# A second-largest expert of 320 rows, and weight remainders split between VectorE and GpSimd

## The chip, the cores and the metric

The kernel runs on one core of one Trainium2 chip. The metric is device time in microseconds of one execution; the times shown are the median of three runs, with their lowest and highest. Traces come from one execution under the hardware profiler.

## The reference

Three layers follow each other, all in float32. Pooled attention turns q, k, v (2 batches, 8 heads, 1152 places, 64 dimensions) into 1152 tokens of 512 numbers. A mixture of experts sends each token to one of 8 experts. A last feed-forward layer has 2048 hidden units.

```python
e_idx = np.argmax(x @ w_gate, axis=1)
gate_w = probs[np.arange(N), e_idx]          # softmax of the logits
eom = 1.0 / (1.0 + np.exp(-(x @ w_output_gate)))
for e in range(E):
    mask = e_idx == e
    h = np.maximum(x[mask] @ w1[e], 0.0)     # 512 -> 1024
    ye = h @ w2[e]                           # 1024 -> 512
    out[mask] = gate_w[mask, None] * eom[mask, e, None] * ye
# last layer, on all tokens
h = x @ w_in                                 # 512 -> 2048
sp = np.where(h > 20.0, h, np.log1p(np.exp(np.minimum(h, 20.0))))
return (h * np.tanh(sp)) @ w_out             # 2048 -> 512
```

With the reference's inputs the eight experts get 374, 267, 240, 69, 63, 61, 51 and 27 tokens, sorted by count.

## The kernel before

The program has four parts in order of time: attention (to about 295 us), the routing (to about 316 us), the experts (to about 467 us) and the last feed-forward layer (to the end). The order of all instructions is the order in which the Python code emits them; each engine works off its own list, and semaphores join the lists.

**Precision.** Most matrix products are made of three matmuls in a fast one-pass format (`float32r`): an operand a is split into a rounded part (hi, by ScalarE) and a remainder (lo, by VectorE or GpSimd: `tt(eng, lo, w, hi, subtract)`), and hi x hi, lo x hi and hi x lo are added up (`mm3`, lines 825 to 827). Where few rows are at stake, plain float32 matmuls are used without a split; the trace records each of them as two.

**Experts.** The experts are ranked by count on the chip, and the program has one slot for each rank. `CAP` gives each rank's room in units of 64 rows: (6, 6, 4, 2, 1, 1, 1, 1). Tokens beyond a slot's room go to up to 9 overflow slots, which run only if needed (none ran in the profiled execution). The slots are visited in the order of ranks 0, 3, 4, 1, 5, 2, 6, 7. Ranks 0, 1, 2 are wide slots (`wide_slot`), the others narrow ones (`narrow_slot`), those of 64 rows with plain float32 matmuls whose two halves of 64 output rows each fill one half of the array (`mm2_half`, line 846).

A wide slot is a pipeline of ten steps. Step i < 8 makes hidden units 128 i to 128 i + 127 for all the slot's rows (12 matmuls, as many columns as the slot has rows, into the tile `hps`, of which there are two), then ScalarE takes the ReLU (`hh`) and VectorE its remainder (`hl`). Step i >= 2 also multiplies hidden tile i - 2 by the second layer, for each column tile of 128 rows three matmuls of 512 columns into its tile `yp`. In each step the weights of a later step are split: `w1h` and `w2h` by ScalarE, `w2l` by VectorE, `w1l` by VectorE for the first three and by GpSimd after that. Besides, in rank 1's slot two parts of the decoding of the last layer's weights (`dm`, `ds`, `wd`) run per step on ScalarE and VectorE, from raw data (`wraw`) that ScalarE's queue fetches. At the end ScalarE evicts `yp` and GpSimd scatters the rows.

The slots' weights come as four loads of 1 MB each (`wt`, line 788) on SP's queue, in order, into five buffers; a load waits for the last reader of the buffer that it takes.

**Last layer.** 48 steps: three blocks b of 384 tokens, 16 tiles f of hidden units. In step i of the loop TensorE makes z of tile i (12 matmuls of 384 columns, `zps`) and the output product of tile i - 4 (9 matmuls of 512 columns, `ops`, line 1265); between them lies the activation, in this order on the engines (offset from i):

```python
order_ = [(-4, z_lo), (-1, z_exp), (-3, z_gate), (-2, z_inv), (-2, z_newton),
          (-1, z_num), (2, split_lo), (-3, z_hi), (3, split_hi)]
```

VectorE's list of a step is thus: gl (`z_lo`), the gate (n from n and `zps` in PSUM), l, l, n (`z_newton`), n from u (`z_num`), and in the first block the remainder of a weight tile (`split_lo`, named wd in the trace since it goes into a buffer of the decoded weights). GpSimd clamps u (`ts(G, u, ...)` in `z_num`); ScalarE does exp, ln, exp, gh and the rounded weight (`split_hi`). The first four weight tiles (`NPRE`) are split during the experts; tiles 4 to 15 in the first block. In steps 8, 10, 12 of a block VectorE also scales a tile of the next block's tokens (yt), and in 9, 11, 13 TensorE transposes it and VectorE takes its remainder (yl, from PSUM).

Before the first step the experts' last results stand in three PSUM banks (`yb`); ScalarE and VectorE split them into yh and yl (`ysplit`). The pools of the last layer's PSUM tiles (`ops`, `zps`, `tps`) are opened after the experts' pools are closed, and take over their banks. A tile pool that is opened with `reuse_waits="tile"` makes a new tile wait for the readers and writers of just the old tile whose place it takes; without it, as these three are here, it waits for more of the closed pool.

Of the kernel before, what the change touches and what calls it, by code (L numbers as in the profile page):

```python
# [20 lines left out]
P = 128  # L21
# [11 lines left out]
CAPW = 3  # L33
CAP = (6, 6, 4, 2, 1, 1, 1, 1)
# [50 lines left out]
def kernel(ctx, tc, cst, qt, kt, v, wgo, w1, w2, wio, out):  # L85
# [824 lines left out]
    def wide_slot(s, cks):  # L910
        n = len(cks) * P

        def xprep(j):
            if j == 0:
                xh[s] = mp_.tile([P, 4, n], F32R, name="xh")
                xl[s] = mp_.tile([P, 4, n], F32R, name="xl")
            ps = xpose(cks[j], *(((yps, "yp") if s == slots[0][0] else (fp[0], f"yb{j - 1}")) if j else ()))
            js = slice(j * P, (j + 1) * P)
            act(xh[s][:, :, js], ps)
            tt(V, xl[s][:, :, js], ps, xh[s][:, :, js].bitcast(F32), ALU.subtract)  # L920
# [13 lines left out]
        def main(i):  # L934
            if i < 8:
                ps = hps.tile([P, 4, P], F32, name="hps").rearrange("p a b -> p (a b)")
                a, b_ = w1s[s, i]
                apart = s == slots[0][0] and i == 0 and n > 256
                if apart:

                    for cs_ in (slice(0, 256), slice(256, n)):
                        for u, x_ in ((a, xh), (b_, xh), (a, xl)):
                            for k in range(4):
                                mm(ps[:, cs_], lhsT=u[:, k], rhs=x_[s][:, k, cs_], start=u is a and x_ is xh and k == 0, stop=x_ is xl and k == 3)
                for k in range(4) if not apart else ():
# [12 lines left out]
    def narrow_slot(s, c, m=P):  # L958
# [32 lines left out]
        def main(i):  # L991
# [75 lines left out]
    allc = [(c, min(P, 64 * CAP[p_])) for p_, cks in slots for c in cks]  # L1067
# [288 lines left out]
```

## Time and profile before

| | us |
|---|---|
| three timed runs: median (lowest to highest) | 695.81 (694.01 to 698.62) |
| the profiled execution: time | 697.16 |
| the profiled execution: span of the trace | 695.4 |
| TensorE matmuls busy | 649.5 (93%) |
| VectorE busy | 523.1 (75%) |
| ScalarE busy | 370.8 (53%) |
| GpSimd busy | 140.1 (20%) |
| mean granted clock of TensorE | 0.981 |

Busy shares are means over stages with different limits; a stage is read from its own stretch of the trace. A row of a timeline gives start, duration, engine, line, operation, output and inputs, shape, count of merged instructions, and in brackets the idle time before it with the engine that ended it. Matmuls overlap, so the distance of two starts is what counts, not the duration.

### The profile page before, as it was taken

The page shows a single profiled execution, that of the slowest core. Times are in us where ns is not written, and L with a number is a line of the kernel's source. Part 1 is how long each engine was busy: PE and PEld are TensorE (multiplying, and loading weights), DVE is VectorE, ACT ScalarE, POOL GpSimd, SP SyncE. Part 2 cuts the span into 40 slices and gives each one's busy share as a digit, 9 for nine tenths or more (in the row PEclk, how much of TensorE's full clock was granted, in tenths as well). Part 3 has the DMA queues.
Part 4 walks back from the last instruction along what each step waited for, and adds up shares of the span by engine and source line. Part 5 has one row for each costly group of instructions (what it writes and reads, how often), then busy time and mean ns, then how long its engine had stood idle before and what let it go on. Part 6 is the DMA issues. An engine that isn't in the chain of part 4 may idle for free. (4 is left out here: it accounts for less than half of the span.)

```text
span 695.4 us, 11495 instructions
## 1 busy us (share of the span) xinstructions
PE 649.5 (93%) x4335; PEld 503.6 (72%) x4335; DVE 523.1 (75%) x1035; ACT 370.8 (53%) x753; POOL 140.1 (20%) x139
## 2 busy tenths in 40 slices
PE   5899999999999999858989999988899999999997
PEld 3666666666767666527876977758688899999995
DVE  6897979797979796965743976613999977897775
ACT  6656474747474737514344546523666554555543
POOL 5310000000000000023222424301222332233322
PEclk9999999999999999969999999998999999999999
DMA  5863544444442303439379878661000020001001
GB/s 207 290 170 107 133 124 123 140 108 146 102 150 64 114 13 124 146 115 341 147 275 374 301 264 315 208 243 46 0 1 1 1 92 1 0 1 47 1 0 46
DMA packets 26641, 88.33 MB, mean 127 GB/s; under 512 B 2886, under 2 KB 7631, under 8 KB 22482
## 3 DMA queue, kind: packets, MB, share of 16 engines
q1 hardware_dynamic: 21264, 73.23, 30.4%
q0 software_dynamic: 3568, 8.79, 5.7%
q10 hardware_dynamic: 1746, 5.51, 2.3%
q8 instruction: 35, 0.57, 0.3%
q14 instruction: 28, 0.23, 0.1%
HBM read 79.65 MB, written 8.39 MB: 127 GB/s over the span
## 5 line engine op out<-in xcount | busy, mean ns | idle before, releaser
L91 ACT ACTIVATE pt<-sc 128x320 f32<-128x320 f32 (+1 forms) x216 | 96.1, 488 | 74.9 <-PE sc L259 70.4
L103 DVE TENSOR_REDUCE Mp<-mx 128x1 f32<-128x384 f32 x198 | 102.0, 547 | 36.8 <-PE mx L215 36.4
L100 POOL TENSOR_SCALAR u<-u 128x384 f32<-128x384 f32 x48 | 59.8, 1246 | 154.0 <-ACT u L91 119.3
L274 PE MATMUL pv<-pt,vt 128*64 128x288 f32 x576 | 85.8, 419 | 3.2 <-PE mx L215 2.1
L215 PE MATMUL mx<-at,qs 128*128 128x384 f32 x176 | 60.9, 392 | 11.4 <-DVE qs L97 7.1
L825 PE MATMUL zps<-yh,wh 128*128 128x384 f32 x188 | 64.5, 343 | 1.7 <-DVE n L97 1.7
L827 PE MATMUL zps<-yl,wh 128*128 128x384 f32 x188 | 63.6, 338 | 0.0
L826 PE MATMUL zps<-yh,wd 128*128 128x384 f32 x180 | 61.2, 340 | 0.0
L1265 PE MATMUL ops<-wh,gl 128*128 128x512 f32 x144 | 57.8, 404 | 3.0 <-DVE gl L94 2.5
L274 PEld LDWEIGHTS pv<-pt,vt 128*64 128x64 f32 x576 | 35.5, 136 | 32.6 <-issue 13.6
L215 PEld LDWEIGHTS mx<-at,qs 128*128 128x128 f32 x176 | 31.8, 194 | 36.3 <-DVE Mp L103 18.9
L1265 PE MATMUL ops<-wh,gh 128*128 128x512 f32 x144 | 56.8, 395 | 0.2 <-ACT gh L91 0.2
L1265 PE MATMUL ops<-wd,gh 128*128 128x512 f32 x135 | 53.1, 394 | 0.0
L91 ACT ACTIVATE l<-n,two 128x384 f32<-128x384 f32 x48 | 29.5, 615 | 25.0 <-DVE n L97 25.0
L97 DVE SCALAR_TENSOR_TENSOR l<-n,r 128x384 f32<-128x384 f32 x48 | 26.6, 554 | 19.9 <-ACT r L91 19.9
L91 ACT ACTIVATE u<-zps 128x384 f32<-128x384 f32 x48 | 23.2, 483 | 33.1 <-PE zps L827 30.4
L825 PEld LDWEIGHTS zps<-yh,wh 128*128 128x128 f32 x188 | 35.7, 190 | 3.6 <-ACT r L91 2.0
L1265 PEld LDWEIGHTS ops<-wh,gl 128*128 128x128 f32 x144 | 27.0, 188 | 13.9 <-DVE gl L94 7.0
L100 DVE TENSOR_SCALAR dm<-dm 128x512 f32<-128x512 f32 x64 | 30.8, 482 | 7.5 <-ACT dm L91 7.4
L91 ACT ACTIVATE gh<-n 128x384 fp32r<-128x384 f32 x48 | 24.8, 517 | 20.6 <-DVE n L97 20.4
L827 PEld LDWEIGHTS zps<-yl,wh 128*128 128x128 f32 x188 | 35.6, 189 | 0.0
L826 PEld LDWEIGHTS zps<-yh,wd 128*128 128x128 f32 x180 | 34.1, 189 | 1.5
(276 smaller groups left out, 1585.1 us busy)
## 6 DMA issues: line engine op xcount, KB each, us to landing
wt<-in_w SPq DMA_DIRECT2D x32, 1024.0 KB, 6.8
wraw<-in_wio SPq DMA_DIRECT2D x23, 512.0 KB, 4.2
kd<-in_kt SPq DMA_DIRECT2D x16, 576.0 KB, 3.9
vt<-in_v SPq DMA_DIRECT2D x8, 576.0 KB, 7.0
wraw<-in_wio ACTq DMA_DIRECT2D x9, 512.0 KB, 6.2
tq<-in_qt SPq DMA_DIRECT2D x12, 288.0 KB, 6.3
tq<-in_qt POOLq DMA_DIRECT2D x12, 288.0 KB, 4.7
pt<-in_qt SPq DMA_DIRECT2D x4, 576.0 KB, 5.1
```

What stands on the lines that cost most here:

```text
L91: A.activation(out=out, in_=in_, func=func, **kw)
L97: V.scalar_tensor_tensor(out=out, in0=a, scalar=s, in1=b, op0=op0, op1=op1)
L100: eng.tensor_scalar(out=out, in0=a, scalar1=s1, scalar2=s2, op0=op0, op1=op1)
L103: V.tensor_reduce(out=out, in_=in_, axis=AX.X, op=op)
L215: mm(ps[:, :384], lhsT=QS[p, h][:, j * P:(j + 1) * P], rhs=At[p, h][:, cs_], start=True, stop=True)
L274: mm(pvt[p][64 * h:64 * h + 64, f, :HQ], lhsT=vt[p][:, t, h, :], rhs=Pt[p, t][:, h, f * HQ:(f + 1) * HQ], start=t == 0, stop=t == KT - 1, ...
L825: mm(out_, lhsT=a, rhs=c, start=first, stop=False)
L826: mm(out_, lhsT=b_, rhs=c, start=False, stop=False)
L827: mm(out_, lhsT=a, rhs=d, start=False, stop=last_)
L1265: mm(opt[b_, j], lhsT=(g_, g_, gl_)[i], rhs=(wo, wl_, wo)[i], start=f == 0 and i == 0, stop=f == NF - 1 and i == 2)
```

## The change

Four edits.

1. `CAP` becomes (6, 5, 4, 2, 1, 1, 1, 1): rank 1's slot holds 320 rows. Its last 64 rows stand as a third, half-filled column tile. Their ReLU is kept in float32 (tile `hn`), and their second layer is made by `mm2_half` from the raw weights (`wt`), not from split ones. First-layer matmuls, ReLU and its remainder shrink with the columns (320 in the first layer, remainder for 256).
2. The routing's small tables of room per rank are worked out from the new numbers (seven small VectorE operations instead of four).
3. In `split_lo`, tiles 4 to 15 are subtracted in two halves of 512 columns, the first by VectorE, the second by GpSimd.
4. The PSUM pools `ops`, `zps` and `tps` are opened with `reuse_waits="tile"`.

```diff
-CAP = (6, 6, 4, 2, 1, 1, 1, 1)
+CAP = (6, 5, 4, 2, 1, 1, 1, 1)
...
-    def mm2_half(s, k, js):
+    def mm2_half(s, k, h_, j=0):
...
         for d in range(2):
-            mm(ypt[s, 0][64 * d:64 * d + 64, :256], lhsT=hh[s, k // 4][:, js], rhs=w[:, 256 * d:256 * d + 256], start=k == 0, stop=k == 7)
+            mm(ypt[s, j][64 * d:64 * d + 64, :256], lhsT=h_, rhs=w[:, 256 * d:256 * d + 256], start=k == 0, stop=k == 7)
...
     def wide_slot(s, cks):
-        n = len(cks) * P
+        n = 64 * CAP[s]
+        cols = [(c, min(P, n - j * P), slice(j * P, min(n, (j + 1) * P))) for j, c in enumerate(cks)]
...
-                relu(s, i, ps[:, :n], n)
+                relu(s, i, ps[:, :n - n % P], n - n % P)
+                if n % P:
+
+                    if i % 4 == 0:
+                        hw.append(mp_.tile([P, 256], F32, name="hn", bufs=2))
+                    hc[i] = hw[-1][:, i % 4 * 64:i % 4 * 64 + 64]
+                    act(hc[i], ps[:, n - 64:n], AF.Relu)
             if i >= 2:
                 k = i - 2
...
+                for j, (c, m, js) in enumerate(cols):
+                    if m == P:
+                        mm2(s, j, k, hh[s, k][:, js], hl[s, k][:, js])
+                    else:
+                        mm2_half(s, k, hc[k], j)
                     if k == 7:
-                        scatter(evac(s, j), six[:, c:c + 1], c)
+                        scatter(evac(s, j) if m == P else evac_half(s, j=j), six[:m, c:c + 1], c)
...
-            tt(eng, lo, wd[f], ws2[f][0].bitcast(F32), ALU.subtract)
+
+            for e_, w in ((V, slice(0, 512)), (G, slice(512, 1024))) if f >= NPRE else ((eng, slice(0, 1024)),):
+                tt(e_, lo[:, w], wd[f][:, w], ws2[f][0].bitcast(F32)[:, w], ALU.subtract)
...
-    ops = ctx.enter_context(tc.tile_pool(name="ops", bufs=3, space=PSUM))
-    zps = ctx.enter_context(tc.tile_pool(name="zps", bufs=4, space=PSUM))
-    tps = ctx.enter_context(tc.tile_pool(name="tps", bufs=1, space=PSUM))
+    ops = ctx.enter_context(tc.tile_pool(name="ops", bufs=3, space=PSUM, reuse_waits="tile"))
+    zps = ctx.enter_context(tc.tile_pool(name="zps", bufs=4, space=PSUM, reuse_waits="tile"))
+    tps = ctx.enter_context(tc.tile_pool(name="tps", bufs=1, space=PSUM, reuse_waits="tile"))
```

How the instructions move, at three places. TensorE, in rank 1's slot, the second layer of an interior step with the last group of the first layer ahead of it; before:

```order
L825 MATMUL hps<-xh,w1h 128x384
L826 MATMUL hps<-xh,w1l 128x384
L827 MATMUL hps<-xl,w1h 128x384
L825 MATMUL yp<-w2h,hh 128x512
L826 MATMUL yp<-w2h,hl 128x512
L827 MATMUL yp<-w2l,hh 128x512
L825 MATMUL yp<-w2h,hh 128x512
L826 MATMUL yp<-w2h,hl 128x512
L827 MATMUL yp<-w2l,hh 128x512
L825 MATMUL yp<-w2h,hh 128x512
L826 MATMUL yp<-w2h,hl 128x512
L827 MATMUL yp<-w2l,hh 128x512
```

The same place with the change (two lines were added above, so line 825 is now 827, and 846 is 848):

```order
L827 MATMUL hps<-xh,w1h 128x320
L828 MATMUL hps<-xh,w1l 128x320
L829 MATMUL hps<-xl,w1h 128x320
L827 MATMUL yp<-w2h,hh 128x512
L828 MATMUL yp<-w2h,hl 128x512
L829 MATMUL yp<-w2l,hh 128x512
L827 MATMUL yp<-w2h,hh 128x512
L828 MATMUL yp<-w2h,hl 128x512
L829 MATMUL yp<-w2l,hh 128x512
L848 MATMUL yp<-wt,hn 64x256 x2
```

Three second-layer matmuls have become two half ones from raw weights, and the first layer has 64 columns less. GpSimd, from the last layer's start to its end; before (u is clamped 48 times, gl comes at the very end):

```order
L1277 MEMSET two 128x1
L100 ISA
L100 TENSOR_SCALAR u<-u 128x384 x48
L94 TENSOR_TENSOR gl<-n,gh 128x384 x2
L1352 UNCONDITIONAL_BRANCH
```

With the change, the same list (of its twelve pairs in the first block the first three):

```order
L1291 MEMSET two 128x1
L99 ISA
L99 TENSOR_SCALAR u<-u 128x384 x2
L93 TENSOR_TENSOR wd<-wd,wh 128x512
L99 TENSOR_SCALAR u<-u 128x384
L93 TENSOR_TENSOR wd<-wd,wh 128x512
L99 TENSOR_SCALAR u<-u 128x384
L93 TENSOR_TENSOR wd<-wd,wh 128x512
```

Each of twelve clamps is now followed by half a weight tile's subtraction. TensorE at the turn into the last layer, with the waits of each instruction (an engine's name with a number is its semaphore); before:

```order
L908 MATMUL yb_5333<-xh 128x128 x4
L908 MATMUL yp<-xh 128x128 x4
L1203 MATMUL zps<-yh,wh 128x384 [waits DVE_49,Activation_49]
L1203 MATMUL zps<-yh,wl_5043 128x384
L1203 MATMUL zps<-yh,wh 128x384
```

With the change:

```order
L910 MATMUL yb_5340<-xh 128x128 x4
L910 MATMUL yp<-xh 128x128 x4
L1217 MATMUL zps<-yh,wh 128x384 [waits PE_49,Activation_49]
L1217 MATMUL zps<-yh,wl_5050 128x384
L1217 MATMUL zps<-yh,wh 128x384
```

The first matmul of the last layer no longer waits for VectorE.

## Rows read from the trace of the kernel before

**Rows 1.** The page, its first line: the span.
```profile
span 695.4 us, 11495 instructions
```

**Rows 2.** Windows: stretch, its length, busy us (instructions) by engine, clock, DMA share, GB/s.
```profile
395.00:412.00 17.00, 17.00 (x86) 14.79 (x85) 15.49 (x30) 7.83 (x15) 2.65 (x2) 1.00 0.72 249
...
467.00:483.00 16.00, 13.46 (x74) 13.00 (x75) 2.66 (x5) 4.01 (x7) 1.29 (x2) 0.79 0.17 56
483.00:535.00 52.00, 48.01 (x237) 40.77 (x235) 50.33 (x81) 34.89 (x59) 14.56 (x12) 1.00 0.00 1
```

**Rows 3.** Timeline of TensorE in the slots of ranks 1 and 2: start us, us.
```profile
394.04 0.39 PE L825 MATMUL yp<-w2h,hh 128*128 128x512 f32 x1
394.27 0.40 PE L826 MATMUL yp<-w2h,hl 128*128 128x512 f32 x1
...
398.23 0.39 PE L825 MATMUL yp<-w2h,hh 128*128 128x512 f32 x1
...
435.63 0.28 PE L825 MATMUL hps<-xh,w1h 128*128 128x256 f32 x1
435.75 0.28 PE L826 MATMUL hps<-xh,w1l 128*128 128x256 f32 x1
```

**Rows 4.** Timeline of TensorE where wide and half matmuls meet.
```profile
376.57 2.81 PE L846 MATMUL yp<-wt,hn 128*64 128x256 f32 x24
...
413.11 0.39 PE L827 MATMUL yp<-w2l,hh 128*128 128x512 f32 x1
413.43 0.87 PE L978 MATMUL hps<-wt,xn 128*64 128x256 f32 x6
...
422.69 0.39 PE L825 MATMUL hps<-xh,w1h 128*128 128x256 f32 x1
422.92 0.28 PE L826 MATMUL hps<-xh,w1l 128*128 128x256 f32 x1
```

**Rows 5.** Timelines of VectorE and TensorE in rank 1's slot: remainder, next use of its buffer.
```profile
390.34 0.55 DVE L97 SCALAR_TENSOR_TENSOR hl<-hps,hh 128x384 fp32r<-128x384 f32 x1
...
391.93 0.33 PE L825 MATMUL hps<-xh,w1h 128*128 128x384 f32 x1
```

**Rows 6.** Timelines of SP's queue and ScalarE: rank 2's first load, a wait for one.
```profile
409.13 0.33 SPq L788 DMA_DIRECT2D wt<-in_w  x1
...
425.54 0.63 ACT L91 ACTIVATE w2h<-wt 128x512 fp32r<-128x512 f32 x1 [0.73 <-DMA wt<-in_w]
```

**Rows 7.** Timelines of ScalarE and TensorE at the turn into the last layer.
```profile
476.14 0.67 ACT L91 ACTIVATE yh<-yp 128x256 fp32r<-128x256 f32 x2
...
477.24 0.41 PE L1203 MATMUL zps<-yh,wh 128*128 128x384 f32 x1 [2.23 <-DVE yl L94]
```

**Rows 8.** Timelines of GpSimd and VectorE in the last layer's first block.
```profile
508.91 1.19 POOL L100 TENSOR_SCALAR u<-u 128x384 f32<-128x384 f32 x1 [3.31 <-ACT u L91]
...
508.99 1.52 DVE L94 TENSOR_TENSOR wd<-wd,wh 128x1024 fp32r<-128x1024 f32 x1
510.44 0.55 DVE L94 TENSOR_TENSOR gl<-n,gh 128x384 fp32r<-128x384 f32 x1
510.91 0.54 DVE L97 SCALAR_TENSOR_TENSOR n<-n,zps 128x384 f32<-128x384 f32 x1
...
513.49 1.52 DVE L94 TENSOR_TENSOR wd<-wd,wh 128x1024 fp32r<-128x1024 f32 x1
...
518.38 1.22 DVE L94 TENSOR_TENSOR wd<-wd,wh 128x1024 fp32r<-128x1024 f32 x1
```

**Rows 9.** Timelines of VectorE and GpSimd in the slots of ranks 1 and 2.
```profile
395.30 0.68 DVE L97 SCALAR_TENSOR_TENSOR ds<-wraw,ds 128x512 int32<-128x512 int32 x1
...
427.34 6.13 POOL L94 TENSOR_TENSOR w1l<-wt,w1h 128x512 fp32r<-128x512 f32 x4 [2.52 <-PE hps L827]
...
430.56 1.78 DVE L97 SCALAR_TENSOR_TENSOR ds<-wraw,ds 128x512 int32<-128x512 int32 x1
432.26 0.41 DVE L97 SCALAR_TENSOR_TENSOR hl<-hps,hh 128x256 fp32r<-128x256 f32 x1
```

More of the change, by code (lines that the diff above doesn't have):

```diff
@@ L32 @@
 TT = NT // P
-CAPW = 3
-CAP = (6, 6, 4, 2, 1, 1, 1, 1)
+CAP = (6, 5, 4, 2, 1, 1, 1, 1)
 NOV = 9
@@ L726, in routing_over @@
         cap, nc9, ov, b8, inc = rt("cap", [8]), rt("nc9", [8, 9]), rt("ov", [8]), rt("b8", [8, 8]), rt("inc", [8])
-        ts(V, cap, pi_, -1.0, ALU.mult, float(CAPW + 1), ALU.add)
-        ts(V, cap, cap, float(CAPW), ALU.min, 0.0, ALU.max)
-        ch, cr = rt("ch", [8]), rt("cr", [8])
+        ch, cr, c5 = rt("ch", [8]), rt("cr", [8]), rt("c5", [8])
         ts(V, ch, pi_, -2.0, ALU.mult, 7.0, ALU.add)
-        ts(V, ch, ch, 5.0, ALU.min, 0.0, ALU.max)
+        ts(V, c5, pi_, -1.0, ALU.mult, 5.0, ALU.add)
+        tt(V, ch, ch, c5, ALU.min)
+        ts(V, ch, ch, 0.0, ALU.max)
+        ts(V, cap, ch, 1.0, ALU.is_ge)
+        stt(cap, ch, 3.0, cap, ALU.is_ge, ALU.add)
+        stt(cap, ch, 5.0, cap, ALU.is_ge, ALU.add)
         ts(V, cr, ch, 64.0, ALU.mult, 64.0, ALU.add)
@@ L832, in mm2, with evac_half @@
         mm3(ypt[s, j], (a, b_), w2s[s, k], k == 0, k == 7)
-    def evac_half(s, y=None, r=0):
+    def evac_half(s, y=None, r=0, j=0):
         y = mp_.tile([P, DM], F32, name="y", bufs=3) if y is None else y
         for d in range(2):
-            act(y[r:r + 64, 256 * d:256 * d + 256], ypt[s, 0][64 * d:64 * d + 64, :256])
+            act(y[r:r + 64, 256 * d:256 * d + 256], ypt[s, j][64 * d:64 * d + 64, :256])
         return y
-    def mm2_half(s, k, js):
+    def mm2_half(s, k, h_, j=0):
         if k == 0:
-            ypt[s, 0] = yps.tile([P, 4, P], F32, name="yp").rearrange("p a b -> p (a b)")
+            ypt[s, j] = yps.tile([P, 4, P], F32, name="yp").rearrange("p a b -> p (a b)")
         w = w2t[s, k // 4][:, k % 4]
         for d in range(2):
-            mm(ypt[s, 0][64 * d:64 * d + 64, :256], lhsT=hh[s, k // 4][:, js], rhs=w[:, 256 * d:256 * d + 256], start=k == 0, stop=k == 7)
+            mm(ypt[s, j][64 * d:64 * d + 64, :256], lhsT=h_, rhs=w[:, 256 * d:256 * d + 256], start=k == 0, stop=k == 7)
     def evac(s, j):
@@ L910, in wide_slot @@
     def wide_slot(s, cks):
-        n = len(cks) * P
+        n = 64 * CAP[s]
+        cols = [(c, min(P, n - j * P), slice(j * P, min(n, (j + 1) * P))) for j, c in enumerate(cks)]
+        hc, hw = {}, []
         def xprep(j):
@@ L916, in xprep @@
                 xl[s] = mp_.tile([P, 4, n], F32R, name="xl")
[L917 to L920, printed above, removed]
+            ps = xpose(cks[j], *(((yps, "yp") if s == slots[0][0] else (fp[0], f"yb{j - 1}")) if j else ()), m=cols[j][1])
+            m, js = cols[j][1:]
+            act(xh[s][:, :, js], ps[:, :, :m])
+            tt(V, xl[s][:, :, js], ps[:, :, :m], xh[s][:, :, js].bitcast(F32), ALU.subtract)
         def pre(i):
@@ L1023, in main @@
                         o = 128 * (k % 2) + 64 * (k % 4 // 2)
-                        mm2_half(s, k, slice(o, o + 64))
+                        mm2_half(s, k, hh[s, k // 4][:, o:o + 64])
                         if k == 1:
@@ L1066 @@
         slots.append((pos_, cks))
-    allc = [(c, min(P, 64 * CAP[p_])) for p_, cks in slots for c in cks]
+    allc = [(c, min(P, 64 * CAP[p_] - P * j)) for p_, cks in slots for j, c in enumerate(cks)]
     load_w(slots[0][0], ei0, 0, (0,))
```

3 lines of the change are left out of this document (removed).

## The prediction

> **What bounds the kernel now.** I read the page first for the span, 695.4 us [rows 1]. The profiled execution itself took 697.16 us, 1.76 us around the span, and lies 1.35 us above the median of the three timed runs (695.81, from 694.01 to 698.62). The sum below is made against 697.16, and 1.35 is taken off at the end.
>
> Then the windows by stage, for the two stretches that the change enters [rows 2]. In the second of the wide slots (395 to 412 us) TensorE is busy 17.00 of 17.00 us at a granted clock of 1.00: TensorE sets the time there, and VectorE is close behind with 15.49. In the first block of the last stage (483 to 535 us) it is the other way round: VectorE is busy 50.33 of 52.00 us and TensorE 48.01, so 3.99 us of TensorE idle lie there. Between them is the turn into the last stage (467 to 483 us), with a mean clock of 0.79, part of it at the lower of the two levels.
>
> Then the timeline, engine by engine, for the step of each stretch. In the wide slot a step is 4.19 us (394.04 to 398.23), second-layer matmuls of 512 columns start 0.23 us apart and first-layer ones of 256 columns 0.12 us apart [rows 3]. In the last stage a step of VectorE is 4.50 us (508.99 to 513.49, between two remainder subtractions) [rows 8]. One step of TensorE there is the same 12 matmuls of 384 and 9 of 512 columns as in the wide slot, hence 4.19 us. So VectorE overhangs by 0.31 us a step.
>
> **Part A: 320 rows instead of 384.** An interior step loses 64 columns of twelve first-layer matmuls and the third column tile's three second-layer matmuls, and gains two float32 half matmuls, which the trace records as four. Old: 9 x 0.23 = 2.07 us for the second layer, so 4.19 - 2.07 = 2.12 for the first. New: between 0.12 us at 256 columns and 0.23 at 512, 320 columns give 0.148, so 12 x 0.148 = 1.77; 6 x 0.23 = 1.38. The half matmuls stand in the narrow slots: 24 records in 2.81 us, 0.117 each [rows 4], so 0.47 for four. Changing the kind of matmul costs too: from the last 512-column one to the first half one 0.32 us pass instead of 0.23, and from half ones back the first wide one takes 0.23 instead of 0.12 [rows 4], together 0.20. New step 1.77 + 1.38 + 0.47 + 0.20 = 3.82, a saving of 0.37. Six steps have both layers (2.22 us), two only the first (0.35 each, 0.70), two only the second (2.07 - 1.38 - 0.67 = 0.02 each): 2.96 us.
>
> Can the others follow? The remainder of the hidden layer for step 2 begins at 390.34 and lasts 0.55; TensorE needs its buffer at 391.93, so the margin is 1.04 us [rows 5]. TensorE will come 2 x 0.35 + 2 x 0.37 = 1.44 us earlier, and VectorE gets 0.55 - 0.41 [rows 5, 9] = 0.14 back on each of three such operations, 0.42: the margin is about 0. Over the slot VectorE needs 15.49 / 17.00 x 4.19 = 3.82 us a step [rows 2], less 0.14. That fits, barely. I take 2.7 of the 2.96 us. Bounds: 2.96, and 1.1 (8 x 0.14) if VectorE sets the step.
>
> The loads move too. The second layer's raw weights are now read by the half matmuls, so the buffer behind the next wide slot's first load comes free only with the slot's last half matmul, not at 409.13 [rows 6]. The end of the slot is at 413.43 [rows 4]; less 2.7 that is 410.7, and the next wide slot begins to use weights 9.26 us after it (413.43 to 422.69). Already now ScalarE waits 0.73 us for a weight there [rows 6]. Queued behind that load on SP are only the three others of that slot. I price this at 0, covered by the narrow slot's matmuls, and at 1 us where that cover is too short. The extra ReLU of 64 columns on ScalarE, three more small routing operations on VectorE and the smaller gather and transposes lie under a full TensorE: 0.
>
> **Part B: pools that wait by tile.** The first matmul of the last stage now waits for VectorE's remainders of the two earlier banks and starts at 477.24 after 2.23 us idle; afterwards it waits for ScalarE's halves, the first of which is done half-way through 476.14 + 0.67 [rows 7]. That is 476.5, and with 0.1 for the signal 476.6: 0.65 us earlier. All that follows starts with it, since the chain from there runs through VectorE. Bounds: 0 and the whole 2.23.
>
> **Part C: the remainders in halves.** In 12 steps VectorE subtracts 512 columns instead of 1,024: 1.22 us where nothing disturbs it, against 0.68 for a two-input operation of 512 columns [rows 8, 9], so it gains 0.54 a step. GpSimd gets the other half, right behind the clamp of u. What does that cost VectorE? The trace has four GpSimd subtractions of 512 columns back to back, 6.13 us, 1.53 each. While they run, a VectorE operation with two inputs in SBUF takes 1.78 us instead of 0.68, 1.10 more, but one that reads PSUM takes its usual 0.41 [rows 9]. So GpSimd's half shuts VectorE out for about 1.1 us unless VectorE is then at an operation on PSUM. The Trainium skill speaks against the split as well: SBUF — State Buffer, section "SBUF: two separate sides", calls the port pair of VectorE and GpSimd an exclusive lock that the first one holds for its whole instruction. By that, the loss would be nearer 1.5 than 1.1; the row shows 1.10, and I use the row.
>
> Where does the hold fall? Take the step from 508.99. GpSimd's clamp runs 508.91 to 510.10, and already stretches VectorE's subtraction by 0.30 (1.52 against 1.22) [rows 8]. In the new step the half (0.30 + about 0.61 to the next start) lets gl begin at 509.90 and end about 510.4; GpSimd asks at 510.1, waits for gl, holds from 510.4 to about 511.5. The gate (n from zps, PSUM) runs through that hold, 0.46 us of it; the next operation, l, wants to start at 510.85 and waits until 511.5, about 0.6. Gained 0.54, lost 0.6: a step of about 4.56 instead of 4.50. Nine steps go so: +0.5 us. In the three steps that carry a scaling of yt between the half and gl, GpSimd gets in ahead of gl, the gate comes too late to cover, and the whole 1.1 is lost: 3 x (1.1 - 0.54) = +1.7. C = +2.2 us. Queued behind the blocked l are all of VectorE's step, and ScalarE's gh and TensorE's output matmuls wait for that; behind the half on GpSimd stands only the next clamp, which comes a step later. Bounds: if the hold costs nothing, VectorE's step is 3.96, TensorE's 4.19 sets the pace, and at most TensorE's idle of 3.99 us comes back; if the gate never covers, 12 x (1.1 - 0.54) = +6.7.
>
> **Sum:** -2.7 - 0.65 + 2.2 = -1.15 us; 697.16 - 1.15 = 696.0, and on the median 694.7.
>
> **Rivals.** *GpSimd's half is free*: it falls where VectorE works on PSUM or idles. For it: GpSimd is idle most of the step, and its start hangs on ScalarE's u, not on VectorE. Against: in a step of 4.50 us VectorE has no idle time and one PSUM operation of 0.46 us, against a hold of 1.1. Then C = -4.0, sum -7.35, 688.5. *The hold is never covered* (the other side): the shifted clamp brings GpSimd's half to the l, l, n operations or ahead of gl in every step, since a delayed l delays the remainder half but not the clamp, which follows the gate by way of ScalarE. Then C = +6.7, sum +3.35, 699.2; it turns from gain to loss when the mean uncovered hold passes 0.54 + 3.35 / 12 = 0.82 us. The Trainium skill's sentence on whole instructions leans to this side. *The slot gives nothing*: the half's rows are served, but VectorE (margin 0) or the late load holds the steps; A = 0, sum +1.55, 697.4. For it: the margin; against: 3.68 of 3.82 us of VectorE work.
>
> **How the numbers follow.** Forecast 0.60 (C from 0 to +4.5: 692.5 to 697.0); free half 0.18; never covered 0.12; slot gives nothing 0.10. About 1%, 7 us, is what a measurement of this kernel can tell from no change. Only the free half, with all of A and B, reaches that: half of its chance, 0.09, to which 0.01 is added for a gain of B's whole bound. Slower by over 1% needs the uncovered hold together with the lost slot: 0.04. The range reaches from just above the free half's time to just above the uncovered hold's, 689.0 to 699.5, and leaves about 2 in 10 out.
>
> **What would show it.** After: a step of the wide slot at 3.8 us (3.7 to 3.9 right; 4.1 means VectorE or switching holds it) with four half records in it; the first last-stage matmul with a wait on ScalarE instead of VectorE, idle before it about 1.6; in the first block VectorE's remainder at 512 columns near 0.68, GpSimd's half between 1.3 and 1.6 us in the shadow of gl and the gate, and the l behind the gate at 1.1 to 1.2 us instead of 0.55. If l stands at 0.55 and TensorE's idle in that stretch is gone, the forecast is wrong by the free half; if gl too stands above 1 us in most steps, by the uncovered hold.

## The result, and the profile after

| | before | after |
|---|---|---|
| median (lowest to highest, 14 runs each), us | 697.06 (693.04 to 699.00) | 703.48 (698.96 to 705.50) |
| ratio, 95% interval | 1 | 1.0084 (1.0064 to 1.0103) |
| span of the profiled execution, us | 695.4 | 699.6 |

The change made the kernel 5.9 us slower (0.0084 x 697). The forecast was 694.7 us, 689.0 to 699.5: the wrong side, and outside the range.

The windows of the profile after, for the three stretches of [rows 2] (columns as there):

```profile
395.00:412.00 17.00, 15.32 (x82) 10.61 (x80) 13.21 (x26) 7.64 (x19) 2.66 (x2) 1.00 0.61 217
467.00:483.00 16.00, 12.39 (x77) 11.73 (x78) 2.24 (x4) 4.19 (x9) 2.29 (x3) 0.89 0.20 63
483.00:535.00 52.00, 45.92 (x220) 39.67 (x219) 50.97 (x76) 32.99 (x56) 30.10 (x22) 0.97 0.00 1
```

In the slot of rank 1 neither TensorE (15.32 of 17.00) nor VectorE (13.21) is full any more, so something there waits. In the first block of the last stage VectorE is as full as before (50.97 of 52), with TensorE at 45.92 instead of 48.01, so the same work of VectorE takes longer there.

Totals are a poor guide to where the time went: the place where rank 1's slot begins lay anywhere between 375.7 and 381.1 us in the seventeen profiled kernels of this study, whose code ahead of it differs in a few small routing operations and the order of some loads at most. So stages are compared by their own length, between two rows of the trace. TensorE's borders after are these: first matmul of rank 1's slot, of the narrow slot behind it, of rank 2's slot, of the next narrow slot, of the last stage:

```profile
377.22 0.41 PE L827 MATMUL hps<-xh,w1h 128*128 128x320 f32 x1
...
412.74 2.76 PE L990 MATMUL hps<-wt,xn 128*64 128x256 f32 x24
...
421.96 0.38 PE L827 MATMUL hps<-xh,w1h 128*128 128x256 f32 x1
...
449.69 2.81 PE L990 MATMUL hps<-wt,xn 128*64 128x256 f32 x24
...
478.40 0.45 PE L1217 MATMUL zps<-yh,wh 128*128 128x384 f32 x1 [1.58 <-ACT yh L90]
```

| stage, us | before | after | difference |
|---|---|---|---|
| rank 1's slot | 34.12 | 35.52 | +1.40 |
| rank 2's slot | 24.80 | 27.73 | +2.93 |
| turn: from the first transpose of yb to VectorE's first gate of the last stage | 16.24 | 14.59 | -1.65 |
| first gate to thirteenth | 54.89 | 58.73 | +3.84 |
| thirteenth gate to the end | 152.10 | 152.29 | +0.19 |

With the two stretches between them (-0.04 and -0.38) that makes +6.3 us, which agrees with the medians.

**Rank 1's slot.** Three engines of the changed kernel in one step, TensorE, ScalarE, VectorE (start us, us, line, operation; in brackets the idle time before it and what ended it):

```profile
391.55 0.39 PE L827 MATMUL yp<-w2h,hh 128*128 128x512 f32 x1
...
393.03 0.65 PE L848 MATMUL yp<-wt,hn 128*64 128x256 f32 x4
394.03 0.42 PE L827 MATMUL hps<-xh,w1h 128*128 128x320 f32 x1 [0.34 <-ACT hn L90]
...
395.89 0.39 PE L827 MATMUL yp<-w2h,hh 128*128 128x512 f32 x1
```

```profile
391.13 0.38 ACT L90 ACTIVATE hh<-hps 128x256 fp32r<-128x256 f32 x1
393.75 0.22 ACT L90 ACTIVATE hn<-hps 128x64 f32<-128x64 f32 x1 [2.24 <-DVE hl L96]
393.87 0.62 ACT L90 ACTIVATE w2h<-wt 128x512 fp32r<-128x512 f32 x1
```

```profile
393.31 0.41 DVE L96 SCALAR_TENSOR_TENSOR hl<-hps,hh 128x256 fp32r<-128x256 f32 x1
394.52 0.69 DVE L93 TENSOR_TENSOR w2l<-wt,w2h 128x512 fp32r<-128x512 f32 x1 [0.81 <-ACT w2h L90]
```

The new ReLU hn (0.22 us) waits 2.24 us for VectorE's hl (0.49 to 2.25 in the seven steps that wait so), although it uses nothing that hl makes. Both read the same tile hps in PSUM, and the program lets the two engines read it one after the other, in the order in which the code emits them: hh, hl, hn. If that is what holds the slot, it is a ring: hn stands in front of w2h on ScalarE; VectorE's w2l waits for w2h (0.81 us, in seven steps); the next hl stands behind w2l; the next hn waits for that hl. TensorE waits at its end, for hn to give hps back. A step takes 4.13 to 4.81 us instead of 4.19 [rows 3]. The Trainium skill has the reason for the order, in PSUM — Partial Sum Buffer, section "PSUM bank collisions raise a hardware error": two engines may not touch one bank and quadrant at once, reads against reads included, and nothing arbitrates, so software must order them. The trace agrees with the wait; no run here shows a collision.

**Rank 2's slot.** Its first load left SP's queue at 412.95 instead of 409.13 [rows 6], and ScalarE waited 3.50 us for weights instead of 0.73. The load that ScalarE waited for, the third, left 4.54 us behind the end of rank 1's slot (4.23 before), but took 10.4 us to land instead of 7.9. SP's queue, then ScalarE:

```profile
412.95 0.33 SPq L790 DMA_DIRECT2D wt<-in_w  x1
```

```profile
427.75 0.63 ACT L90 ACTIVATE w2h<-wt 128x512 fp32r<-128x512 f32 x1 [3.50 <-DMA wt<-in_w]
```

**First block.** VectorE in a step without yt, and in a pair of steps with yt and yl (compare [rows 8]); then GpSimd in the same steps:

```profile
506.20 0.68 DVE L93 TENSOR_TENSOR wd<-wd,wh 128x512 fp32r<-128x512 f32 x1
506.80 0.55 DVE L93 TENSOR_TENSOR gl<-n,gh 128x384 fp32r<-128x384 f32 x1
507.27 0.54 DVE L96 SCALAR_TENSOR_TENSOR n<-n,zps 128x384 f32<-128x384 f32 x1
507.74 1.19 DVE L96 SCALAR_TENSOR_TENSOR l<-n,r 128x384 f32<-128x384 f32 x1
...
510.81 0.68 DVE L93 TENSOR_TENSOR wd<-wd,wh 128x512 fp32r<-128x512 f32 x1
...
516.01 0.47 DVE L99 TENSOR_SCALAR yt<-yt,gsc 128x512 f32<-128x512 f32 x1
516.40 1.61 DVE L93 TENSOR_TENSOR gl<-n,gh 128x384 fp32r<-128x384 f32 x1
...
520.52 0.69 DVE L93 TENSOR_TENSOR wd<-wd,wh 128x512 fp32r<-128x512 f32 x1
...
522.34 0.54 DVE L96 SCALAR_TENSOR_TENSOR n<-n,zps 128x384 f32<-128x384 f32 x1
522.81 1.66 DVE L96 SCALAR_TENSOR_TENSOR l<-n,r 128x384 f32<-128x384 f32 x1
```

```profile
505.18 1.35 POOL L99 TENSOR_SCALAR u<-u 128x384 f32<-128x384 f32 x1 [1.27 <-ACT u L90]
507.03 1.48 POOL L93 TENSOR_TENSOR wd<-wd,wh 128x512 fp32r<-128x512 f32 x1 [0.50 <-DVE wd L93]
...
516.24 1.37 POOL L93 TENSOR_TENSOR wd<-wd,wh 128x512 fp32r<-128x512 f32 x1 [0.50 <-DVE wd L93]
521.50 1.17 POOL L99 TENSOR_SCALAR u<-u 128x384 f32<-128x384 f32 x1 [3.90 <-ACT u L90]
522.75 1.30 POOL L93 TENSOR_TENSOR wd<-wd,wh 128x512 fp32r<-128x512 f32 x1
```

A plain step is 510.81 - 506.20 = 4.61 us (4.50 before), with l behind the gate at 1.19 instead of 0.55. In the steps with yt the hold hits gl (1.61), and in those with yl it hits l, uncovered (1.66): GpSimd's half begins at 522.75, when the gate (to 522.88) is nearly over. From gate to gate such a pair took 9.68 us before and 10.46, 10.82 and 10.81 after.

### The profile page after: what moved, and what is told of

It is laid out like the page before. It is cut to its first block, busy times and chain, and to the rows that moved or that the text cites. A ratio compares the mean times of both kernels' runs of the same rounds, so it can differ in the third digit from the quotient of the medians.

```text
span 699.6 us, 11531 instructions
## 1 busy us (share of the span) xinstructions
PE 645.3 (92%) x4343; PEld 495.7 (71%) x4343; DVE 525.4 (75%) x1038; ACT 371.0 (53%) x762; POOL 158.7 (23%) x151
## 5 line engine op out<-in xcount | busy, mean ns | idle before, releaser
L99 POOL TENSOR_SCALAR u<-u 128x384 f32<-128x384 f32 x48 | 61.5, 1282 | 131.5 <-ACT u L90 99.5
L214 PE MATMUL mx<-at,qs 128*128 128x384 f32 x176 | 60.6, 390 | 11.3 <-DVE qs L96 8.6
L96 DVE SCALAR_TENSOR_TENSOR l<-n,r 128x384 f32<-128x384 f32 x48 | 32.7, 680 | 19.8 <-ACT r L90 19.8
L301 POOL COPY xu<-xu 128x64 f32<-128x64 f32 x8 | 3.0, 370 | 160.0 <-ACT xu L90 160.0
L93 DVE TENSOR_TENSOR w2l<-wt,w2h 128x512 fp32r<-128x512 f32 x32 | 25.6, 804 | 16.8 <-ACT w2h L90 15.2
```

Source lines behind the costliest of these rows:

```text
L93: eng.tensor_tensor(out=out, in0=a, in1=b, op=op)
L96: V.scalar_tensor_tensor(out=out, in0=a, scalar=s, in1=b, op0=op0, op1=op1)
L99: eng.tensor_scalar(out=out, in0=a, scalar1=s1, scalar2=s2, op0=op0, op1=op1)
L214: mm(ps[:, :384], lhsT=QS[p, h][:, j * P:(j + 1) * P], rhs=At[p, h][:, cs_], start=True, stop=True)
L301: G.tensor_copy(xu4[:, hp, 64 * b:64 * b + 64], xu[:, o:o + 64])
```

## The experiments

All stage lengths, each from one profiled execution, with medians and ratios where the kernel was timed beside before:

| kernel | rank 1's slot | rank 2's slot | turn | gates 1 to 13 | median | ratio (95%) |
|---|---|---|---|---|---|---|
| before | 34.12 | 24.80 | 16.24 | 54.89 | | 1 |
| after | 35.52 | 27.73 | 14.59 | 58.73 | 703.48 | 1.0084 (1.0064 to 1.0103) |
| e1_cap | 35.42 | 26.86 | 16.29 | 54.91 | 700.45 | 1.0050 (1.0029 to 1.0071) |
| e2_halves | 34.11 | 24.17 | 16.58 | 58.72 | 701.33 | 1.0053 (1.0025 to 1.0080) |
| e3_reuse | 34.25 | 25.93 | 14.15 | 54.91 | 694.26 | 0.9948 (0.9914 to 0.9981) |
| e4_hn_first | 31.69 | 27.65 | 16.25 | 54.90 | 697.56 | 0.9990 (0.9968 to 1.0013) |
| e12_after_hn | 32.14 | 27.18 | 14.56 | 58.78 | 700.13 | 1.0039 (1.0019 to 1.0059) |
| e5_mm3 | 31.79 | 25.74 | 16.26 | 54.91 | 696.77 | 0.9986 (0.9960 to 1.0013) |
| e9_late | 34.29 | 25.37 | 16.29 | 54.89 | | |
| e13_hold_both | 31.92 | 27.73 | 16.25 | 54.89 | | |
| e14_hold_last | 32.21 | 28.08 | 16.30 | 54.90 | | |
| e6_swap | 31.45 | 23.91 | 16.29 | 54.90 | 694.47 | 0.9954 (0.9922 to 0.9986) |
| e8_dummy | 34.11 | 24.18 | 15.71 | 65.54 | | |
| e7_quarter | 34.20 | 25.25 | 14.92 | 55.23 | 699.45 | 1.0017 (0.9986 to 1.0049) |
| e10_best | 31.46 | 24.17 | 14.16 | 54.89 | 689.92 | 0.9896 (0.9878 to 0.9914) |
| e11_best_q | 31.45 | 23.85 | 14.30 | 55.02 | 691.40 | 0.9918 (0.9891 to 0.9945) |
| e15_best_q10 | 31.45 | 24.00 | 14.31 | 54.05 | 691.17 | 0.9919 (0.9885 to 0.9952) |

Rank 1's slot and the gates repeat within 0.15 us between kernels with the same code there (0.45 between e4_hn_first and e12_after_hn). Rank 2's slot waits for loads and varies: 24.17, 24.18, 24.80, 25.25 and 25.93 in the five kernels whose expert code is that of before, 24.9 on the mean.

### The parts alone

**e1_cap**: `CAP` and the routing's table, nothing else of the change (its first two edits).

> Edits 1 and 2 alone: rank 1 holds 320 rows, its last 64 through hn and the raw weights; remainders and pools as before. Theory (a ring): hn, on ScalarE, waits for VectorE's hl, since both read the same PSUM tile; w2h stands behind hn, w2l of VectorE behind w2h, the next hl behind w2l. So the slot takes about 35.5 us from its first matmul to the next slot's, not 34.1, VectorE idles 0.8 us a step in front of w2l, and the weights of rank 2 come about 2 us late: 4.3 us slower in all, 701.4. Rival (the loss of the whole change is the last stage's alone): 694.4 to 697.

Measured: 35.42 and 26.86 us in the two slots, 3.5 us slower (0.0050 x 697). The slot theory holds, 0.8 us short of its size.

**e2_halves**: the split of `split_lo` alone.

> Edit 3 alone: the remainders in halves. Theory (GpSimd's half shuts VectorE out): steps of 4.6 us in the first block, pairs of steps with yt and yl of 10.8 us instead of 9.7, 3.0 us slower, 700.1. Rival (the loss seen there in the changed kernel came from the late slots or the other pools): within 0.5 us of before.

Measured: 58.72 us, step for step as in the changed kernel; 3.7 us slower. The loss of the last stage is the halves' own.

**e3_reuse**: `reuse_waits="tile"` on `ops`, `zps` and `tps` alone.

> Edit 4 alone. Theory: TensorE idles 1.58 us instead of 2.23 ahead of the first matmul of the last stage, and the whole is 0.65 us faster; in the changed kernel the clock was granted in full right behind that matmul (windows: 0.89 instead of 0.79 in 467 to 483 us), which would add up to 1 us: 696 to 697.3 where before is 697.95. Rival (what follows waits for something else): the same time, the first gate as far behind the end of the experts as before.

Measured: 1.58 us idle ahead of the first matmul, as forecast, and the turn 2.1 us shorter. The ratio says 3.6 us (1.3 to 6.0); the stages account for 2.1. The other 1.4 us of the turn go with the clock (last section).

### Rank 1's slot: the ring, or the engines' work?

**e4_hn_first**: the first two edits, with one block moved.

```diff
+                if n % P:
+                    ...
+                    act(hc[i], ps[:, n - 64:n], AF.Relu)
                 relu(s, i, ps[:, :n - n % P], n - n % P)
-                if n % P:
-                    ...
-                    act(hc[i], ps[:, n - 64:n], AF.Relu)
```

> Edits 1 and 2, but hn is issued ahead of hh, so that it waits for TensorE alone and hl waits for both. Theory (the ring): VectorE's wait in front of w2l is gone, a step of the slot is 3.8 to 3.9 us, the slot about 31.4 to 32 us; the load of rank 2's weights still comes only with the slot's last half matmul, which costs about 2.2 us of it: 696.5, with 695 to 697.5. Rival (the half matmuls and the change of kind are dear themselves): steps stay at 4.1 us or more and the time at 700 or above. Rival (VectorE's own work holds the slot): steps of 4.0 to 4.2 with VectorE without idle time.

TensorE in one step of e4_hn_first, then VectorE in the next step:

```profile
386.02 0.39 PE L827 MATMUL yp<-w2h,hh 128*128 128x512 f32 x1
...
387.50 0.65 PE L848 MATMUL yp<-wt,hn 128*64 128x256 f32 x4
388.08 0.41 PE L827 MATMUL hps<-xh,w1h 128*128 128x320 f32 x1
388.34 0.30 PE L828 MATMUL hps<-xh,w1l 128*128 128x320 f32 x1
...
389.94 0.39 PE L827 MATMUL yp<-w2h,hh 128*128 128x512 f32 x1
```

```profile
391.41 0.41 DVE L96 SCALAR_TENSOR_TENSOR hl<-hps,hh 128x256 fp32r<-128x256 f32 x1
391.75 0.68 DVE L93 TENSOR_TENSOR w2l<-wt,w2h 128x512 fp32r<-128x512 f32 x1
```

The step is 3.92 us, no wait stands in it, and w2l follows hl at once. Moving a ReLU of 0.22 us ahead of the remainder takes 3.7 us off the slot (35.42 to 31.69): the ring is shown. Both rivals fall. Rank 2's slot kept its loss, and the whole came out at before's time, within 0.3%.

**e12_after_hn**: the same move in the whole changed kernel.

> The changed kernel whole, with hn issued ahead of hh. Theory: its slot of rank 1 takes 31.5 to 31.9 us instead of 35.5, rank 2's slot stays at 27 to 28 with the late load, the first block at 58.7 from the first gate to the thirteenth: 3.5 us less than the changed kernel, 699 to 700. Rival (the ring was hidden by what follows): within 1 us of the changed kernel's 703.5.

Measured: 32.14 us in the slot, 700.13 in all, a ratio to before of 1.0039 where the change has 1.0084. The ring cost the changed kernel some 3 us.

**e5_mm3**: 320 rows, but no half matmul in the slot: one ReLU and remainder of 320 columns, and for the last 64 rows

```diff
-                    if m == P:
-                        mm2(s, j, k, hh[s, k][:, js], hl[s, k][:, js])
-                    else:
-                        mm2_half(s, k, hc[k], j)
+                    mm2(s, j, k, hh[s, k][:, js], hl[s, k][:, js], m)
```

where `mm2` writes to the first m partitions.

> 320 rows without half matmuls: the last 64 rows' hidden units are split as all others are (hh and hl of 320 columns), and their second layer takes three matmuls of 512 columns onto 64 partitions, from the split weights. So nothing waits for hn, no kind of matmul changes, and the load of rank 2's weights waits for w2l as before. Theory: a step of 1.76 + 9 x 0.23 = 3.83 us, the slot 2 to 2.9 us shorter than before, the next slots as before: 694.2 to 695. Rival (VectorE holds the slot whatever TensorE has to do): step 4.1, 696.5 or more.

TensorE in one step of e5_mm3 (128\*64 is a matmul with 64 output partitions):

```profile
390.08 0.39 PE L827 MATMUL yp<-w2h,hh 128*128 128x512 f32 x1
...
391.47 0.40 PE L827 MATMUL yp<-w2h,hh 128*64 128x512 f32 x1
...
392.16 0.31 PE L827 MATMUL hps<-xh,w1h 128*128 128x320 f32 x1
...
393.92 0.39 PE L827 MATMUL yp<-w2h,hh 128*128 128x512 f32 x1
```

A step takes 3.84 us (one in the slot took 4.16, where TensorE waited for VectorE's hl). The three split matmuls of the last column tile take 392.16 - 391.47 = 0.69 us. In e4_hn_first the half block with its two changes of kind takes 0.58 up to the next start, 0.09 more ahead of it and 0.11 behind it, 0.78. So the half matmuls save TensorE nothing. The time, 696.77 us, missed the 694.2 to 695 that were written down: the slot gained 2.3 us as expected, but the ratio shows 1.0 us (2.8 less to 0.9 more), and does not resolve so little; rank 2's slot, at 25.74, is inside before's spread.

### Rank 2's slot: late loads, or the half matmuls?

**e9_late**: before, with a matmul of 64 columns at the end of rank 1's slot that reads the last raw buffer.

```diff
                     if k == 7:
+                        if s == 1 and j == len(cks) - 1:
+                            pd = hps.tile([P, 4, P], F32, name="hps").rearrange("p a b -> p (a b)")
+                            mm(pd[:, :64], lhsT=ident, rhs=w2t[s, 1][:, 3, :64], start=True, stop=True)
```

> The kernel before, with one matmul of 64 columns at the end of rank 1's slot that reads the second half of its second layer's raw weights into a tile that nobody reads. It holds back rank 2's first load from some 4.3 us ahead of the slot's end to the end, and does nothing else. Theory (the late load is what lengthens rank 2's slot in e1_cap and e4_hn_first): ScalarE waits about 3 us for w2h, and rank 2's slot takes 26.8 to 27.8 us instead of 24.2 to 25.9; slot of rank 1 as before, 34.1 to 34.4. Rival (it is something else in the edit): below 25.9.

Measured: the load left SP at 413.57, 0.09 us behind the slot's end, as meant; ScalarE waited 1.32 us and the slot took 25.37 us. By what was written down this was for the rival: a late load behind a slot of full length costs no more than the spread.

**e13_hold_both**, **e14_hold_last**: e5_mm3, with such matmuls at hidden tiles 3 and 7, or at 7 alone.

```diff
+                    if m < P and k in (3, 7):
+                        mm(ypt[s, j][64:, :64], lhsT=hh[s, k][:, :64].bitcast(F32), rhs=w2t[s, k // 4][:, k % 4, :64], start=True, stop=True)
```

> As e5_mm3 (320 rows, all split, no half matmul in the second layer's work), but two matmuls of 64 columns read the two raw second-layer buffers where the last half matmul of each would have read it (hidden tiles 3 and 7) and write to partitions that nobody uses. So both buffers come free as late as in e4_hn_first, and nothing else is taken over from it. Theory (in e4_hn_first rank 2's slot took 27.65 us, not 25.74, because the loads behind come late): rank 2's slot 27 to 28 us, ScalarE waiting about 3 us for w2h. Rival (the half matmuls or hn themselves do it): 25.2 to 26.2 as in e5_mm3.

> As e13_hold_both with the second of the two matmuls alone (hidden tile 7): only rank 2's first load is late. In e9_late that alone, behind a slot of full length, gave 25.4 us, inside the spread of the kernel before (24.2 to 25.9). Theory (the one late load is enough once the slot ahead is 2.4 us shorter): 27 to 28 us. Rival (it takes both buffers): 25.5 to 26.5.

ScalarE's waits for rank 2's weights in e14_hold_last:

```profile
416.64 1.15 ACT L90 ACTIVATE w1h<-wt 128x512 fp32r<-128x512 f32 x2 [1.23 <-DMA wt<-in_w]
...
423.57 0.63 ACT L90 ACTIVATE w2h<-wt 128x512 fp32r<-128x512 f32 x1 [3.52 <-DMA wt<-in_w]
```

27.73 and 28.08 us, against 25.74 in e5_mm3. In e14_hold_last one buffer held back to the slot's end is enough; hn and the half matmuls aren't needed for it. Why did the same hold cost so little in e9_late? The third load, the one that w2h needs, left 5.26 us behind the slot's end there, 4.34 in e14_hold_last and 4.23 in before, but took 7.4, 11.1 and 7.9 us to land; e9_late, then e14_hold_last (KB, us from issue to landing):

```profile
wt<-in_w SPq DMA_DIRECT2D x1, 1024.0 KB, 7.4
wt<-in_w SPq DMA_DIRECT2D x1, 1024.0 KB, 11.1
```

The DMA engines are as busy in the 14 us behind the slot's end in before as in e14_hold_last (a share of 0.97 in both), and the loads land one behind the other (in e1_cap at 421.1, 424.5 and 427.8). So what is still due when the third load leaves holds it up, and two things can be. One is the first load: before had moved 1.03 MB on SP's queue in the 4 us ahead of the slot's end, e9_late, e1_cap and e14_hold_last next to nothing. The other is ScalarE's last fetch of raw data (`wraw`, 0.5 MB): in the 4 us behind the end its queue moved 0.49 MB in before, 0.01 in e9_late, 0.52 in e1_cap and 0.48 in e14_hold_last. So before and e9_late have one of the two late, e1_cap and e14_hold_last both; and as the slot ahead was long in e1_cap (35.42), a shorter slot is not the condition. ScalarE began w2h 11.3 to 13.3 us behind the slot's end in the five kernels with before's expert code, after 12.7 in e9_late, 13.1 in e5_mm3, 14.1 in e1_cap and 15.5 in e14_hold_last, and rank 2's slot has the same order. That fits, but no run moved the fetch by itself.

**e6_swap**: e5_mm3, with the four loads of a wide slot in another order.

```diff
-                load_w(slots[n_ + 1][0], ej, slots[n_ + 1][0])
+                load_w(slots[n_ + 1][0], ej, slots[n_ + 1][0], (0, 2, 1, 3) if len(slots[n_ + 1][1]) > 1 else (0, 1, 2, 3))
```

> As e5_mm3 (320 rows, all split), and the four loads of a wide slot are issued in the order first layer 0, second layer 0, first layer 1, second layer 1, so that rank 2's first second-layer weights are asked for one load earlier. In e5_mm3 the slot of rank 1 was 2.3 us shorter (31.79 for 34.12), the slot of rank 2 0.9 us longer (25.74 for 24.80), with ScalarE waiting 1.67 us for that load. Theory (what a shorter slot gains is partly given back in the wait for the loads behind it): that wait is gone, rank 2's slot takes 24.8 us or less, the whole 1 us less than e5_mm3, 2 to 2.5 less than before: 695.5. Rival (the transfers are limited by what moves in all, not by their order): slot of 25.5 to 26, another weight is waited for.

Measured: no wait for w2h, 23.91 us in rank 2's slot, 31.45 in rank 1's; 3.2 us faster than before (1.0 to 5.4).

### The last stage: what is a half on GpSimd worth?

**e8_dummy**: before, with GpSimd's half as extra work.

```diff
             tt(eng, lo, wd[f], ws2[f][0].bitcast(F32), ALU.subtract)
+            if f >= NPRE:
+                dmy = zo.tile([P, 512], F32R, name="dmy")
+                tt(G, dmy, wd[f][:, 512:], ws2[f][0].bitcast(F32)[:, 512:], ALU.subtract)
```

> The kernel before, with VectorE's remainders whole, and beside them GpSimd's subtraction of 512 columns into a tile that nobody reads: the price of the hold without the gain. Theory: the gain of halves is 12 x 0.54 = 6.5 us and the net loss in e2_halves 3.8 (58.72 for 54.89 from the first gate to the thirteenth), so the hold costs 10.3 us there: about 65.2 us. Rival (halves lose by order or by waits, not by GpSimd's running): below 57.

VectorE, then GpSimd, in one step of e8_dummy:

```profile
509.92 1.52 DVE L94 TENSOR_TENSOR wd<-wd,wh 128x1024 fp32r<-128x1024 f32 x1
511.37 1.62 DVE L94 TENSOR_TENSOR gl<-n,gh 128x384 fp32r<-128x384 f32 x1
```

```profile
511.11 1.47 POOL L94 TENSOR_TENSOR dmy<-wd,wh 128x512 fp32r<-128x512 f32 x1
```

65.54 us, 10.65 more than before (10.3 expected): GpSimd's running alone costs more than the halves gain, and the rival falls. That the sums agree so well is in part luck, since the hold falls elsewhere here. A step is 5.57 us, 1.07 more than before, where in e2_halves the hold cost 0.64 (0.54 gained, 0.10 lost); the first two pairs with yt and yl lost 1.0 and 1.8, against 1.9 and 2.2. The 1.07 us are gl's, which could go on only 0.14 us ahead of the end of GpSimd's operation (511.37 + 1.62 - 0.55 = 512.44; 511.11 + 1.47 = 512.58).

**e7_quarter**: before, with VectorE at 768 and GpSimd at 256 columns of tiles 4 to 15.

> Edit 3 alone with another size: VectorE subtracts 768 columns of a remainder, GpSimd 256. Theory (GpSimd's hold goes with its size, and the gate from PSUM covers 0.46 us of it): a hold of about 0.5 us, VectorE gains 0.27 a step and loses 0 to 0.2; steps without yt 4.3 to 4.45 us instead of 4.50, from the first gate to the thirteenth 53 to 55 us instead of 54.9: 696 to 698. Rival (a hold has a length of its own, about 1 us, whatever the size): steps above 4.8, 701 or more.

Measured: plain steps 4.31 us, but pairs with yt and yl 9.76, 10.13 and 10.14; 55.23 us from the first gate to the thirteenth, and the whole within 0.5% of before. The hold goes with the size: 0.53 us where nothing covers it (gl 1.08 instead of 0.55), 0.08 behind the gate.

**e11_best_q**: on e10_best (below), 256 columns on GpSimd except for tiles 10, 12 and 14. **e15_best_q10**: for tiles 4 to 10 only.

> As e10_best, and remainders of the last stage's tiles split 768 columns on VectorE and 256 on GpSimd, but not in the three steps that carry a scaling of yt, where VectorE takes all 1,024. In e7_quarter a step without yt took 4.31 us instead of 4.50, but a step with yt 5.24 to 5.63 instead of 4.9, since GpSimd got in ahead of gl. Theory: from the first gate to the thirteenth 53.0 to 54.0 us instead of 54.9, 1 to 1.8 us less than e10_best. Rival (what is gained in one step is waited for in the next, on ScalarE or TensorE): 54.5 or more.

> As e10_best, and GpSimd takes 256 of 1,024 columns of the remainders of tiles 4 to 10 only. In e11_best_q GpSimd's part of a tile ran a step ahead of VectorE's: its parts of tiles 11, 13 and 15 fell into the steps with yt and stretched gl from 0.55 to 1.08 us. Left out here. Theory: steps of 4.31 us instead of 4.50 before the first yt, of 4.9 and 4.8 behind it as before: 53.8 to 54.2 us from the first gate to the thirteenth (54.89 in e10_best), 0.7 to 1.1 us less in all. Rival: what VectorE gains is waited for elsewhere, 54.6 or more.

e11_best_q missed: 55.02 us. GpSimd's part of a tile runs right behind its clamp and VectorE's at the step's end, so that the parts under the scalings of yt were those of tiles 11, 13 and 15, which had been left in. e15_best_q10 leaves them out: 54.05 us, 0.84 less, as forecast. VectorE, then GpSimd, in a step of e15_best_q10:

```profile
497.83 0.54 DVE L96 SCALAR_TENSOR_TENSOR n<-n,zps 128x384 f32<-128x384 f32 x1
498.30 0.63 DVE L96 SCALAR_TENSOR_TENSOR l<-n,r 128x384 f32<-128x384 f32 x1
...
500.50 1.26 DVE L93 TENSOR_TENSOR wd<-wd,wh 128x768 fp32r<-128x768 f32 x1
```

```profile
497.59 0.92 POOL L93 TENSOR_TENSOR wd<-wd,wh 128x256 fp32r<-128x256 f32 x1 [0.30 <-DVE wd L93]
```

The gate hides all but 0.08 us of the hold. The medians do not show the 0.84 us: e15_best_q10 and e10_best overlap.

### What the parts are worth together

**e10_best**: e6_swap and the pools by tile; remainders as before.

> 320 rows all split, the wide slots' loads in the order of e6_swap, and the last layer's pools waiting by tile (edit 4). Theory: the parts add up: slot of rank 1 31.5 to 31.8 us (34.1 before), of rank 2 about 24 (24.2 to 25.9 in runs whose code there is that of before), the first last-stage matmul after 1.58 us idle: 4 to 6 us faster, 692.5 to 694.5 where before is 698. Rival (the gains share one cover, as both end in the turn): no more than e6_swap alone, 694.5 to 695.5.

Measured: 689.92 us, 7.2 less than before (6.0 to 8.5), more than the 4 to 6 that were written down, and the fastest kernel here with e15_best_q10. Its stages account for 5.4 of it (2.7, 0.6 and 2.1); the rest is not placed.

## Why the prediction was wrong

**Part A, the step of 3.82 us: right as TensorE's own work, wrong as the step.** Freed of the ring, a step took 3.92; the difference is the change of kind of matmul, 0.31 a step where 0.20 was taken. The slot then gave back 2.43 us, where 2.7 were taken. The step that failed is the sentence that put the extra ReLU of 64 columns under a full TensorE at 0. Its own 0.22 us did lie there; its wait was not looked at. The prediction counted VectorE's margin and took ScalarE as free, but an instruction added to a queue that works in order also brings what it waits for. The built order, which the prediction read on TensorE, had it on ScalarE in all eight steps:

```
L90 ACTIVATE hh<-hps 128x256 [waits PE]
L90 ACTIVATE hn<-hps 128x64 [waits DVE]
```

So -2.7 became +1.4. The margin of hl's buffer, on which the rival "the slot gives nothing" rested, played little part: in e4_hn_first the steps shown have no such wait, and in e5_mm3 one step lost 0.32 us to VectorE (TensorE's next group starts at 388.23, hl ends at 388.17).

**Part A, the loads: mechanism right, size wrong.** The lateness was seen (first load at the slot's end), its price was put at 0, or 1 at most, with the narrow slot's matmuls as cover. It cost 2 to 3 us (e13_hold_both, e14_hold_last, 27.7 and 28.1 for 25.7). The cover of 9.26 us was measured against one load, but the one that is waited for is the third, and it lands behind the first two: ScalarE begins w2h 15.0 us behind the slot's end (427.75 - 412.74) instead of 12.1.

**Part B: right, and under a third of it.** The wait moved from VectorE to ScalarE and from 2.23 to 1.58 us [rows 7], 0.65 as worked out. The turn became 2.1 us shorter in e3_reuse, close to the upper bound of 2.23, for a reason that was not in the sum, the clock, so that this nearness is luck.

**Part C: mechanism right, one kind of step mis-sized.** Forecast +2.2, measured +3.84. Plain steps came at 4.60 (4.56 worked out), with l at 1.19 (1.1 to 1.2), and gl in the steps with yt lost 1.06 (1.1). But the steps with yl were taken for plain ones: there the clamp comes 0.98 us behind VectorE's half of the remainder (521.50, 520.52), not 1.02 ahead of it (505.18, 506.20), GpSimd's half starts behind the gate, and l loses all of 1.1. The three pairs lost 0.78, 1.14 and 1.12 us instead of 0.62. The first step, at 4.89, lost 0.39 that wasn't expected. Nor was what the halves cost ahead of the first gate: there n, which took 0.56 us before, took 1.54 beside GpSimd's first half (485.74 and 485.45). The turn is 0.44 us longer than in e3_reuse (14.59, 14.15), so that part C is 4.3 us in all. The Trainium skill's sentence on the exclusive lock that the first one holds for its whole instruction (SBUF — State Buffer, section "SBUF: two separate sides") agrees with the rows here better than the 1.10 us of [rows 9] that were taken as the hold's length: what VectorE loses is nearly all that remains of GpSimd's subtraction when VectorE's next operation on SBUF comes up, 1.07 of 1.47 us in e8_dummy. That holds for a scaling of yt with one input too (1.49 us instead of 0.47 there). The sentence does not fit GpSimd's clamp of u: a subtraction of VectorE that starts 0.08 us behind it takes 0.30 longer [rows 8], and is not shut out for the clamp's 1.19.

**The chances.** No rival had the slot slower than before: the worst case for A was 0. With +1.4 and the loads at +2.9 instead, the other terms as they were forecast give 697.16 + 1.4 + 2.9 - 0.65 + 2.2 - 1.35 = 701.7, already above the range. A bound on A from the side of a loss needed only one question: what may the new instruction wait for, and what stands behind it?

## What to carry to other kernels

An added instruction is priced by its duration, by what it waits for, and by what waits behind it in its engine's queue; the built order with its waits shows the second before any run, and where two engines read one PSUM tile, the order of the readers is a choice: here the short one, with w2h behind it, had to go first (35.42 to 31.69 us). A saving that makes a stage shorter also makes the transfers behind it late, so that loads are to be ordered by when each is needed, and a buffer whose last reader moves to the stage's end is not free. Work given to GpSimd beside a full VectorE pays only as far as VectorE is then at PSUM, and the pieces have to be cut to that (256 columns under a gate of 0.46 us, not 512).

## What the hardware showed that was not expected

**The clock behind the turn.** The granted clock of the 5 us that begin with the last stage's first matmul, from the windows of e6_swap (pools as before, TensorE idle for 2.23 us ahead of it) and of the changed kernel (1.58 us):

```profile
470.75:475.75 5.00, 5.00 (x20) 5.00 (x21) 0.45 (x1) 1.59 (x3) 0.50 (x1) 0.66 0.01 3
```

```profile
478.40:483.40 5.00, 5.00 (x28) 5.00 (x29) 1.86 (x4) 3.09 (x6) 1.19 (x1) 1.00 0.00 0
```

TensorE gets through 20 matmuls in the one and 28 in the other, since in the first the clock is at its lower level (1.2 of 2.4 GHz) for a part of the stretch (0.66 on the mean). It fell so in 9 of the 11 profiled kernels that idled 2.23 us there, and in none of the 6 that idled 1.58. That goes with 1.4 us of the turn beside the 0.65 of the wait (2.1 in e3_reuse). e7_quarter and e8_dummy idled 2.23 us and kept the full clock, so the wait alone does not decide it.

**Half matmuls.** On 64 of 128 output partitions a split matmul of 512 columns takes the same 0.23 us as on 128 (e5_mm3), and four float32 half matmuls with their changes of kind take 0.78 us, more than the three split ones they replace (0.69).
